# The last row of decays of blocks 0 to 3, stored and loaded back through GpSimd's DMA queue instead of SyncE's

## The chip, the cores and the metric

The kernel runs on one core of one Trainium2 chip. A core has TensorE (PE in the profile) for matrix products, VectorE (DVE), ScalarE (ACT), GpSimd (POOL) and SyncE (SP), which issues DMAs, and 16 DMA engines which move the data. Each engine works through its own instructions in program order and waits at semaphores for the others. Times are device microseconds of one execution; a kernel's time is the median of its runs.

## The reference

Gated linear attention, one step at a time, and then a feed-forward layer with a squared ReLU on its output:

```python
# q, k, v, alpha: (4, 8, 768, 48) float32, alpha in 0.8 to 1.0
for t in range(S):
    state = alpha[:, :, t, :, None] * state + einsum('bhd,bhe->bhde', k[:, :, t], v[:, :, t])
    y[:, :, t] = einsum('bhd,bhde->bhe', q[:, :, t], state)
x = y.transpose(0, 2, 1, 3).reshape(3072, 384)
h = maximum(x @ w_in, 0.0)        # w_in (384, 2048)
out = (h * h) @ w_out             # w_out (2048, 384)
```

The two weight matrices arrive as float64.

## The kernel before

**Blocks.** The sequence of 768 steps is cut into 6 chunks of 128, for 4 batch entries: 24 blocks, numbered n = 4c + b for chunk c of batch entry b. A block holds 128 steps by 8 heads by 48 channels. Its steps in the program have short names. `load` brings in alpha, q, k and v (line 109, 192 KB each). `ln` takes the logarithm of alpha on ACT (line 244); `cs` sums it along the chunk by a matmul with a triangle (line 265); `eb` and `ei` (lines 276 and 280, ACT) give b, the decay from the start of the chunk to each step, and its inverse; `mq` and `mk` multiply q by b and k by the inverse (line 284, DVE). `qT`, `kT` transpose on PE, `qc`, `kc` copy the results out of PSUM. `sc` makes the scores (line 372) and `kv` the sums of k and v (line 395) on PE; `am` masks the scores (line 380) and `us` adds the state (line 406) on DVE. `ya` and `yb` are the two halves of the output y of two blocks (line 352, PE); `ev` copies y into x (line 515, DVE and ACT in turn).

**The last row.** The next chunk's state is the sum so far times the last row of b, channel by channel. That row lies along one partition and is needed as columns, one channel per partition. So it goes through memory: `bl` (line 297) stores the row of 384 floats, 1.5 KB, into a small DRAM tile `row`; `br` (line 303) loads it back in two DMAs of 48 x 4 single floats each (0.8 KB) into the tile `last`, which has room for four blocks. `st` (lines 420 and 421, DVE) uses it: line 421 multiplies by `last`. All 20 blocks that have a successor do this, and all of these DMAs are issued by SP, among its loads. b has two buffers, so `eb` of block n waits until `bl` of block n-2 is done reading.

**Order.** The kernel is scheduled by hand. Blocks 0 to 3 (GB = 4) follow a list of step names (lines 851 to 860); each engine's program has them in the order of the list. The part with the first `bl` and `br`:

```python
ln0 cs0 ei0 mk0 warm0 eb0 bl0 mq0 kT0 load0v kc0 ln1 qT0 load2a load2k cs1
eb1 qc0 mq1 sc0 bl1 kv0 qT1 load1v ei1 mk1 load2q load3a kT1 ln2 qc1 load3k
cs2 br0 am0 kc1 eb2 sc1 weights0 br1 us0 kv1 zeros2 bl2 load2v am1 ei2 us1
load3q ya0 ln3 cs3 yb0 eb3 weights1 mk2 ei3 load3v mq2 qT2 st0 ev0 kT2
```

`zeros` are matmuls without use that fill PE's waits. `weights` loads an eighth of a weight matrix (line 126 or 130, 768 KB); `first`, `middle`, `second` convert it from float64 on DVE (lines 153, 157; 175, 179, 182) and ACT (lines 166, 169). `ha` and `hb` are the first feed-forward matmuls (line 805). The other blocks are woven into the feed-forward work by cost and due time; the feed-forward matmuls are at lines 622, 701 and 805.

**Queues.** SP's DMAs take eight semaphores in turn, so a DMA of SP is issued only when the one eight places before it has landed. GpSimd has memsets and masks at the start (to line 212, `last`) and then carries only a wait between `ya` and `yb` (line 456): it waits for the end of `ya`'s matmuls and then lets `yb` begin.

Of the kernel before, what the change touches and what calls it, by code (L numbers as in the profile page):

```python
# [17 lines left out]
GB = 4  # L18
# [7 lines left out]
def kernel(  # L26
# [12 lines left out]
    nc = tc.nc  # L39
    B, H, S, D = q.shape  # L40
    C = 128
# [171 lines left out]
    last_t = [last[:, i, :] for i in range(4)]  # L213
    dram = ctx.enter_context(tc.tile_pool(name="dram", bufs=1, space=bass.MemoryType.DRAM))
    rows_t = [dram.tile([1, H * D], FP32, name=f"row{n}") for n in range(NBLK)]
# [14 lines left out]
    blk = [{} for _ in range(NBLK)]  # L230
# [51 lines left out]
    def scaled(x, n, factor):  # L282
        t = tile_of(x, n)[:, :, 0:D]
        nc.vector.tensor_tensor(
            out=t, in0=t, in1=factor.rearrange("a (h d) -> a h d", h=H), op=ALU.mult
        )
# [4 lines left out]
    def mk(n):  # L291
        scaled("k", n, blk[n].pop("inv"))

    def bl(n):

        if n // B < NCH - 1:
            nc.sync.dma_start(out=rows_t[n], in_=blk[n]["b"][C - 1 : C, :])

    def br(n):
        if n // B < NCH - 1:  # L300
            row = rows_t[n].rearrange("a (p e d) -> (a d) e p", e=2, d=D)
            for e in range(2):
                nc.sync.dma_start(out=last_t[n % 4][64 * e : 64 * e + D, :], in_=row[:, e])  # L303

    def turned(x, n):
        rows = tile_of(x, n).rearrange("a h d -> a (h d)")
# [530 lines left out]


    steps = {f.__name__: f for f in (ln, sp, cs, eb, ei, mq, mk, bl, br, qT, qc, kT, kc, ev)}
    steps["sc"], steps["kv"], steps["am"] = scores, state_sums, masked  # L840
    steps["us"], steps["st"] = sums_copied, next_state
# [132 lines left out]
    for g in range(1, NG):  # L974
        events = []
        if g + 1 < NG:
            n = GB * (g + 1) + 2
# [4 lines left out]
        if g == 1:  # L982
# [5 lines left out]
            n = min(AT["k0"], AT["k1"])  # L988
# [41 lines left out]
```

## Time and profile before

| | us |
|---|---|
| median of 3 runs (522.41 to 522.86) | 522.62 |
| span of the profiled execution, first to last instruction | 520.6 |
| PE busy | 510.8 |
| DVE busy | 366.0 |
| ACT busy | 313.0 |
| POOL busy | 5.4 |

The profile is one execution. "Busy" is the sum of an engine's instructions; SPq and POOLq in the timelines are the queues of SP and POOL, in which the issue of a DMA or a wait is an instruction of its own. A timeline line gives the start, the length, the engine, the line of the kernel, the operation and what it writes and reads; in brackets is the engine's idle time just before it and what ended it. The chain of work goes back from the last instruction to whatever released each step. A matmul's end is modelled, not measured.

### The profile page before, as it was taken

How to read it: one execution, taken by the hardware profiler on the slowest of the kernel's cores; microseconds unless marked ns; L12 is line 12 of the kernel's file. 1: busy time of each engine (PE TensorE's matmuls, PEld its weight loads, DVE VectorE, ACT ScalarE, POOL GpSimd, SP SyncE). 2: the span in 40 equal slices, each digit the busy share in tenths (PEclk: the TensorE clock that was granted, in tenths of full speed). 3: DMA queues.
4: the chain of work that ended last, by engine and by line, in shares of the span. 5: the costliest groups of instructions: out<-in, count | busy, mean ns of one | idle time of the engine just before them, and what ended most of it. 6: DMA issues, size and time to landing. Idle time of an engine off the chain costs nothing.

```text
span 520.6 us, 12925 instructions
## 1 busy us (share of the span) xinstructions
PE 510.8 (98%) x5276; PEld 418.2 (80%) x5276; DVE 366.0 (70%) x631; ACT 313.0 (60%) x650; POOL 5.4 (1%) x29
## 2 busy tenths in 40 slices
PE   7989999999999999999999999999999999999997
PEld 4754455668887668988899988899988899988997
DVE  4798989979978787867597476587465476363861
ACT  4668785677888594575963275963275763164620
POOL 4000000000000000000000000000000000000000
PEclk9999999999999999999999999999999999999999
DMA  9999687244686787898884788964673534898201
GB/s 161 209 278 213 196 240 218 60 114 176 224 200 196 195 246 198 264 317 206 195 248 148 251 246 198 230 187 150 231 255 126 179 126 151 268 340 293 70 0 62
DMA packets 140995, 102.36 MB, mean 197 GB/s; under 512 B 111476, under 2 KB 114568, under 8 KB 140936
## 3 DMA queue, kind: packets, MB, share of 16 engines
q1 hardware_dynamic: 140936, 101.53, 68.3%
q8 instruction: 42, 0.69, 0.6%
q14 instruction: 17, 0.14, 0.1%
HBM read 84.18 MB, written 17.33 MB: 195 GB/s over the span
## 4 chain that ended last, share of the span: by engine, by line
PE 93%; DVE 2%; SPq 2%; DMA 1%; issue 1%; POOL 1%; ACT 0%; POOLq 0%; DVEq 0%
PE o L701 41%; PE h L622 32%; PE h L805 7%; PE y L352 4%; PE T L482 2%; PE sckv L372 2%; PE sckv L395 2%; PE cs L265 1%; DMA qk_lent<-in_q_dram 1%; SPq L303 1%; SPq L109 1%; PE cs L268 1%; PE cs L269 1%; DVE x L515 0%; DVE w_in L182 0%
## 5 line engine op out<-in xcount | busy, mean ns | idle before, releaser
L622 PE MATMUL h<-xa,wb 128*128 128x512 f32 x240 | 68.2, 392 | 0.0
L622 PE MATMUL h<-xl,wl 128*128 128x512 f32 x240 | 67.9, 391 | 0.0
L622 PE MATMUL h<-xd,wd 128*128 128x512 f32 x240 | 67.3, 396 | 0.0
L515 ACT COPY x<-y 32x256 f32<-32x256 f32 (+2 forms) x132 | 47.2, 366 | 25.4 <-PE y L352 20.1
L547 DVE TENSOR_TENSOR hid<-h,hid 128x512 f32<-128x512 f32 x40 | 27.6, 689 | 45.5 <-PE h L622 45.4
L701 PE MATMUL o<-wb,ha 128*128 128x384 f32 x160 | 54.6, 342 | 0.0
L701 PE MATMUL o<-w_out,hid 128*128 128x384 f32 x160 | 54.0, 491 | 0.0
L701 PE MATMUL o<-wd,hd 128*128 128x384 f32 x304 | 53.8, 334 | 0.0
L701 PE MATMUL o<-wl,hl 128*128 128x384 f32 x160 | 53.5, 335 | 0.0
L639 ACT ACTIVATE h<-h 128x512 f32<-128x512 f32 x40 | 23.3, 582 | 49.7 <-PE h L622 49.7
L622 PEld LDWEIGHTS h<-xl,wl 128*128 128x128 f32 x240 | 45.1, 188 | 10.0 <-DVE xl L547 0.4
L701 PEld LDWEIGHTS o<-wd,hd 128*128 128x128 f32 x304 | 52.7, 188 | 0.3 <-DVE osb L737 0.3
L622 PEld LDWEIGHTS h<-xa,wb 128*128 128x128 f32 x240 | 44.6, 188 | 9.3 <-ACT xa L596 0.2
L622 PEld LDWEIGHTS h<-xd,wd 128*128 128x128 f32 x240 | 44.2, 188 | 9.2
L701 PE MATMUL o<-wb,hx 128*128 128x384 f32 x144 | 48.7, 338 | 0.0
L701 PE MATMUL o<-wl,hx 128*128 128x384 f32 x144 | 48.1, 334 | 0.0
L701 PEld LDWEIGHTS o<-w_out,hid 128*128 128x128 f32 x160 | 29.8, 190 | 19.3
L637 ACT ACTIVATE hid<-h 128x512 f32<-128x512 f32 x40 | 24.0, 600 | 34.6 <-PE h L622 34.5
L805 PE MATMUL h<-x,w_in 128*128 128x512 f32 (+1 forms) x108 | 43.6, 552 | 1.2 <-ACT x L515 1.2
L596 ACT ACTIVATE ha<-hid 128x512 fp32r<-128x512 f32 x40 | 25.6, 639 | 25.5 <-DVE hx L547 16.1
L805 PEld LDWEIGHTS h<-x,w_in 128*128 128x128 f32 x108 | 19.9, 190 | 21.1 <-issue 17.2
L547 DVE TENSOR_TENSOR hl<-hid,ha 128x512 fp32r<-128x512 f32 x40 | 27.5, 688 | 10.1 <-ACT ha L596 10.1
(114 smaller groups left out, 879.7 us busy)
## 6 DMA issues: line engine op xcount, KB each, us to landing
wd<-do SPq DMA_DIRECT2D x36, 384.0 KB, 3.7
wl<-lo SPq DMA_DIRECT2D x34, 384.0 KB, 4.0
wl<-li SPq DMA_DIRECT2D x32, 384.0 KB, 3.5
wd<-di SPq DMA_DIRECT2D x32, 384.0 KB, 3.9
raw<-in_moe_w_in_dram SPq DMA_DIRECT2D x8, 768.0 KB, 5.6
raw<-in_moe_w_out_dram SPq DMA_DIRECT2D x8, 768.0 KB, 5.6
v_in<-in_v_dram SPq DMA_DIRECT2D x24, 192.0 KB, 4.7
out_dram<-osb SPq DMA_DIRECT2D x24, 192.0 KB, 1.9
```

Of the source, the lines that this page charges most:

```text
L352: ins = nc.tensor.matmul(out=ys[e][64 * half : 64 * half + D + G * e, m % 2, p // 2, t], lhsT=lhsT, rhs=rhs, start=(half, e) not in seen, ...
L372: nc.tensor.matmul(out=ps[e][HALF[h], 0, p, :], lhsT=ks[rows, p, HALF[h]], rhs=qs[rows, p, HALF[h]], start=True, stop=True, skip_group_che ...
L395: nc.tensor.matmul(out=ps[h][64 * e : 64 * (e + 1), 1, p, G:64], lhsT=tile_of("k", n)[HALF[h], 2 * p + e, :], rhs=tiles["v"][n % NV][HALF[ ...
L482: nc.tensor.transpose(out=ps[h][:, i, p, :], in_=rows[HALF[h], 128 * p : 128 * (p + 1)], identity=ident[HALF[h], HALF[h]],)
L515: copy(out=x[kk][to : to + m, t : t + 2], in_=blk[n]["y"][e][r : r + m, :, p // 2],)
L547: nc.vector.tensor_tensor(out=o, in0=x, in1=z, op=op)
L596: nc.scalar.activation(out=a, in_=x, func=AF.Copy, scale=NEAR)
L622: nc.tensor.matmul(out=acc["h", j], lhsT=here[w, "i", p][:, kk, jj * 128 : (jj + 1) * 128], rhs=x_parts[x][:, kk], start=start and kk == 0 ...
L637: nc.scalar.activation(out=hid[j], in_=x, func=AF.Copy, scale=E)
L639: nc.scalar.activation(out=x, in_=x, func=AF.Copy, scale=1.0 + E)
L701: nc.tensor.matmul(out=acc[t][:, 0:DM], lhsT=lhs[:, t * C : (t + 1) * C], rhs=rhs, start=start, stop=stop, skip_group_check=True,)
L805: nc.tensor.matmul(out=ps, lhsT=w[:, kk, c0 : c0 + 128], rhs=xT[g][kk][:, cols], start=(kk == 0), stop=(kk == KM - 1),)
```

## The change

`queue(n)` is GpSimd's queue for blocks 0 to 3 and SP's for the others; `bl` and `br` issue through it. Blocks 4 to 19 are as before, and so is the order of every other instruction on every engine.

```diff
+    def queue(n):
+        return nc.gpsimd if n < GB else nc.sync
+
     def bl(n):
 
         if n // B < NCH - 1:
-            nc.sync.dma_start(out=rows_t[n], in_=blk[n]["b"][C - 1 : C, :])
+            queue(n).dma_start(out=rows_t[n], in_=blk[n]["b"][C - 1 : C, :])
 
     def br(n):
         if n // B < NCH - 1:
             row = rows_t[n].rearrange("a (p e d) -> (a d) e p", e=2, d=D)
             for e in range(2):
-                nc.sync.dma_start(out=last_t[n % 4][64 * e : 64 * e + D, :], in_=row[:, e])
+                queue(n).dma_start(out=last_t[n % 4][64 * e : 64 * e + D, :], in_=row[:, e])
```

In GpSimd's program the order becomes: memset of `last`; bl0, bl1; br0 (two DMAs), br1 (two); bl2; the wait between ya0 and yb0; br2 (two); bl3; br3 (two); the wait between ya2 and yb2; then the other waits as before. Each `br` waits for its block's `bl` to land, each `bl` for ACT's `eb`. In the changed program bl is cut into 16 pieces of 24 floats, where SP's was one piece of 384.

## The prediction

> **What bounds the kernel now.** I read the page first, then the chain of work up to 90 us in order of time, then the timelines of DVE, SP and PE up to 40 us, then the DMA rates of those 40 us.
>
> The page:
>
> ```profile
> span 520.6 us, 12925 instructions
> PE 510.8 (98%) x5276; PEld 418.2 (80%) x5276; DVE 366.0 (70%) x631; ACT 313.0 (60%) x650; POOL 5.4 (1%) x29
> PE 93%; DVE 2%; SPq 2%; DMA 1%; issue 1%; POOL 1%; ACT 0%; POOLq 0%; DVEq 0%
> ```
>
> PE is busy for 510.8 of 520.6 us, so 9.8 us of idle PE are all that any reordering can win. The table by stretches puts 5.1 us of them before 35 us (PE 29.90 of 35.00); from 35.29 us on the chain is PE matmuls end to end, except one gap of 0.96 us at 203.09 us, called "issue". So the change can only win by bringing forward the moment at which PE starts its unbroken run, and everything moved lies before that moment. The chain there, in order of time (start, length, what):
>
> ```profile
> 9.45 0.25 SPq L297
> ...
> 13.12 2.31 SPq L303
> ...
> 18.25 5.06 DMA qk_lent<-in_q_dram
> 23.31 0.02 issue
> 23.33 0.10 DVE qk_lent L284
> ...
> 34.87 0.37 ACT x L515
> 35.25 0.04 issue
> 35.29 9.72 PE h L805 x26
> ```
>
> This looks as if the row transfers on SP (L297, L303) delay the load of block 3's q, and that load the whole start. DVE's timeline tells how much of it counts (start, length; idle before it and what ended it in brackets):
>
> ```profile
> 17.86 0.36 DVE L421 TENSOR_TENSOR s<-s,last 128x192 f32<-128x192 f32 x1 [1.41 <-DMA last<-row]
> 18.87 2.65 DVE L515 COPY x<-y 32x256 f32<-32x256 f32 x6 [0.65 <-PE y L352]
> ...
> 23.33 0.56 DVE L284 TENSOR_TENSOR qk_lent<-qk_lent,b 128x384 f32<-128x384 f32 x1 [0.28 <-DMA qk_lent<-in_q_dram]
> ```
>
> From 18.87 to 34.05 us DVE hardly stops. It waits 0.28 us for q3. **The bound of this stretch is DVE's run from 18.87 us**, so two things count: that 0.28 us, and what starts the run. The run starts after PE's y matmuls (18.12), which stand behind cs3 (PE 17.27, idle 0.47 before it, ended by ACT's logarithm of alpha of block 3), which waited for that load (ACT 16.70, idle 2.95, DMA).
>
> SP and the DMA rates (40 slices of 1 us):
>
> ```profile
> 4.43 1.15 SPq L109 DMA_DIRECT2D k_in<-in_k_dram  x1
> 6.89 0.31 SPq L297 DMA_DIRECT2D row<-b  x1
> 7.24 0.38 SPq L109 DMA_DIRECT2D v_in<-in_v_dram  x1
> ...
> 13.12 2.79 SPq L303 DMA_DIRECT2D last<-row  x2
> GB/s 0 13 218 206 191 192 187 157 132 223 204 182 193 187 185 92 15 143 356 331 233 122 122 324 377 221 214 244 376 288 196 351 346 238 101 142 358 393 360 364
> ```
>
> Loads run at about 190 GB/s, 1.0 us for each 192 KB. SP is stopped twice by the moved transfers. From 5.58 to 6.89 it waits for eb0; the load of v0 goes out only at 7.24, and the rate falls to 157 and 132 GB/s in the slices of 7 and 8 us. From 13.1 to 17.8 SP issues rows while the queue behind runs dry: 92 and 15 GB/s in the slices of 15 and 16 us.
>
> **The change part by part.** Twelve DMAs leave SP: 4 stores (L297, median 0.28 us of issue) and 8 loads (L303, median 0.44 us, together 5.6 us). POOL gets the same twelve behind its last memset, which ends at 6.21; after that POOL has no compute. No instruction of PE, DVE or ACT changes place.
>
> (1) v0 goes out at 5.6 instead of 7.24, so its data follow the sixth load without a gap. The gap is the shortfall of two slices: (190-157)/190 + (190-132)/190 = 0.48 us. The queue is full from there to 15 us, so v0, a2, k2, v1, q2, a3 and k3 all land some 0.5 us earlier. PE stood idle 0.45 us for v0 (10.31) and ACT 1.54 us for a2 (11.35). Link by link: kv0 9.8, qT1 10.4, kT1 10.9, cs2 11.4 (was 11.92), zeros 13.6, first half of y 15.1 to 16.3 (was 16.80), cs3 16.75 (was 17.27), second half 17.6, DVE's run 18.37. Gain 0.5 us. It can't be much more: mq1 and mk1 (9.46, 9.93) hang on eb1, which nothing moves. Bounds: 0.2 (half the gap is filled) and 0.55.
>
> (2) q3 lands earlier. The weights behind k3 start some 2 us sooner (no slices of 92 and 15 GB/s), so q3 lands near 20.5 instead of 23.31, when DVE is still in its copies. That takes 0.28 us off DVE. The rest of the chain's 5.06 us is worth nothing, because DVE was busy beside it. Next in line is L179, which needs ACT's L169 (ended 24.18, moves to 23.68): it would start at 23.9, so the 0.28 stays.
>
> (3) L421's wait for "last" (1.41 us) lay under the wait for PE's y and is worth nothing by itself.
>
> (4) On POOL I call T the mean time that one of these DMAs holds POOL. No row of this trace shows GpSimd issuing a DMA. The nearest is the same transfer on SP, 0.44 us; the ends are SP's shortest issue of it, 0.30, and its longest, 3.98 (that one waited). I take 0.44. The landing after the issue is taken as 2.0 us (row 3: issue ended 25.18, next L303 at 27.32; last of block 0: 15.91 to 17.86). Two deadlines: block 0's columns are there at 9.42+3T+2.0, needed at 18.0, so T may be 2.2. Block 3's end a chain of eleven DMAs after eb1 with two stores waited for: 9.42+11T+2x2.1+2.0 = 15.6+11T, needed by DVE's L421 at 36.87-0.78 = 36.1, so T may be 1.86. At 0.44 both are hidden, with nothing to pay. ACT's eb2 and eb3 now wait for POOL's stores, long landed by then (9 and 12 us against 12.9 and 17.7).
>
> The Trainium skill, DMA: Bandwidth & Descriptors, section "Latency and other measured facts", gives about 1 us to the first byte when GpSimd generates descriptors in software, against some 600 ns from SP; T of 1 would be an estimate by that page, and the sum stays the same by it. No run so far shows it.
>
> (5) The waits that GpSimd carries between the two halves of y (L456, 0.017 us each, the first at 16.9) now stand behind bl2 and br3 in POOL's program. The first of them releases PE's second half. If it waits for the seven DMAs before it, 9.42+6T must be below 16.4, so T may be 1.16; if it is done beside them, it costs nothing. At 0.44 neither costs.
>
> **Sum**: 0.5 + 0.28 = 0.78 us off the profiled 520.6, 519.8 us of span. The median of the runs shown is 522.62, 2.0 above the span; I carry the difference over: **521.8 us**. PE's clock row is 9 throughout, so clock plays no part.
>
> **Rivals.** *GpSimd's issue is slow (slower than before).* If T passes 1.86, each further 0.1 us of T brings block 3's columns 1.1 us late; DVE holds at L421 with the weight conversions behind it, which feed PE's L805. At T = 2.2 the columns land at 39.8, 3.7 us late, of which the waits of DVE on ACT at 42 to 52 us (0.53, 0.56, 1.20) give back some: about 523.5 to 525. At 2.5, 7 us late, up to 528. For it: these loads are 192 pieces of 4 bytes each, and nothing here shows how software handles them. Against it: it needs four times SP's time. With (5) in the strict form the loss starts at T of 1.16, and at T = 1.5 DVE's run starts 2.0 us later than forecast: 523.8.
> The Trainium skill, SBUF — State Buffer, section "SBUF: two separate sides", says that GpSimd cannot write descriptors while DVE runs an operation in a two-port mode; this would be part of this rival.
> Here L153 and L157 do 768 elements in 0.555 us where L284 takes 0.556 for 384; if such pairs (at 21.5 and 27.2) hold POOL, it is 2x1.1 us in all, and the limit for T falls from 1.86 to 1.66.
>
> *More is won.* The gap of 0.96 us at 203 us has no releaser; if it falls elsewhere and closes, 0.78+0.96 gives 520.9. It may also open elsewhere.
>
> *The transfers are hidden anyway.* If the lagging engine sets a3's landing, (1) wins nothing: the packet records show one 16 KB instruction packet of 1.46 us at 13.46, and a3's last part about 1.3 us behind the others. Then 0 to 0.28 is left: 522.3 to 522.6.
>
> **How the numbers follow.** 0.2% is 1.05 us, about what a measurement of this kernel can tell from no change. Forecast (0.3 to 1.05 us off, 521.6 to 522.3): 0.40. Hidden anyway: 0.13. More won, over 1.05 us: 0.25. Slow issue, slower by over 1.05 us: 0.22. So faster 0.25, same 0.53, slower 0.22. The range takes in the closed gap (520.9, rounded out to 520.8) and the slow issue up to T of some 2.3 (525.5); about 0.15 is left out, most of it above.
>
> **What would show it.** (1) right: no dip of the rate at 7 to 9 us, kv0 near 9.8, cs3 near 16.8, DVE's copies near 18.4. (2) right: no DMA wait ahead of DVE's L284 of q3, and L805's unbroken run near 34.5. (4) right: POOL's rows for the twelve DMAs below 1.8 us, block 0's columns landed before 17, L421 without a DMA wait near 36. Wrong: DVE idle at L421 for "last", or PE's second half of y waiting for POOL.

## The result and the profile after

The changed kernel takes **525.99 us** (five runs, 524.34 to 526.21) beside 522.62 us: a ratio of 1.0048, 95% interval 1.0036 to 1.0059. It is slower by 3.4 us, where 0.8 us less was forecast. Its profiled execution took 526.21 us with a span of 524.4 us, 3.8 us more than the span before. The lines of the code move: what was 297, 303, 352, 421, 456, 515 and 805 is now 300, 306, 355, 424, 459, 518 and 808.

The page of the changed kernel, the lines that were shown of before:

```profile
span 524.4 us, 12935 instructions
PE 512.2 (98%) x5276; PEld 420.3 (80%) x5276; DVE 365.7 (70%) x631; ACT 312.9 (60%) x650; POOL 12.2 (2%) x41
PE 93%; DVE 2%; SPq 2%; DMA 1%; issue 1%; ACT 0%; POOLq 0%; DVEq 0%
```

PE is idle for 12.2 us instead of 9.8, and busy for 1.4 us more with the same 5276 matmuls. So two things went wrong: PE stood still, and some of its work ran slower. Busy time that grows with no work added points at the clock.

The chain of waits of the changed kernel, in order of time (start, length, what):

```profile
11.03 5.90 DMA a_lent<-in_alpha_dram
16.93 0.02 issue
16.95 0.53 ACT a_lent L244
...
29.35 0.68 PE y L355 x28
30.03 1.65 issue
31.68 0.92 PE y L355 x16
...
33.83 14.04 PE h L808 x36
47.86 0.64 PE cs L265 x2
```

Before, the same cs stood at 45.01. The new thing is the 1.65 us in the middle of the y matmuls: "issue" says that PE waited for nothing that the profile shows. Here is PE's timeline at that place, first before and then after:

```profile
29.73 1.49 PE L352 MATMUL y<-am,v_in 64*48 64x64 f32 x64
```

```profile
29.61 0.42 PE L355 MATMUL y<-am,v_in 64*48 64x64 f32 x13
31.68 2.14 PE L355 MATMUL y<-am,v_in 64*48 64x64 f32 x51 [1.65 <-issue]
```

Up to the gap nothing is lost. DVE's timeline of the changed kernel:

```profile
17.27 0.36 DVE L424 TENSOR_TENSOR s<-s,last 128x192 f32<-128x192 f32 x1 [0.65 <-DMA last<-row]
19.12 2.65 DVE L518 COPY x<-y 32x256 f32<-32x256 f32 x6 [1.50 <-PE y L355]
...
23.22 0.55 DVE L284 TENSOR_TENSOR qk_lent<-qk_lent,b 128x384 f32<-128x384 f32 x1
...
33.88 2.67 DVE L518 COPY x<-y 32x256 f32<-32x256 f32 x6 [1.86 <-PE y L355]
```

Its first copies start 0.25 us later than before (18.87), the wait for q3 is gone, and its run reaches 32.03, some 0.1 us ahead of before. There it waits 1.86 us for the y that PE did not make: its second copies are 1.71 us late (33.88 against 32.17).

After that the same work takes longer. Here is PE's busy time in stretches of 3.413 us, laid along the steps in which this profile's clock changes (stretch; length, PE busy and its matmuls, granted clock, DMA share, GB/s):

```profile
24.65:28.06 3.41, 3.27 (x135) 1.00 0.71 186
28.06:31.48 3.42, 1.62 (x48) 1.00 1.13 304
31.48:34.89 3.41, 3.10 (x54) 0.50 1.03 195
34.89:38.30 3.41, 3.41 (x10) 0.50 0.88 290
38.30:41.72 3.42, 3.42 (x14) 1.00 0.99 262
```

The granted clock halves at 31.48, right after the stretch with the gap, and stays so for 6.83 us, two such stretches. In the profile of before it is 1.00 from 5.90 us to near the end. PE resumes at 31.68, so the y matmuls behind the gap ran at half clock too: 51 of them took 2.14 us, where the same 51 take 1.36 us at full clock (run 1 below). So of the 1.71 us some 0.93 belong to the gap and 0.78 to the clock, an estimate from these two rows. The count for the profiled execution: 0.93 us from the gap, 0.78 from the clock in y, 1.14 more until cs at 47.86 (2.85 in all; in runs 1, 2, 4, 5, 6 and 7, at full clock, cs shifts as DVE's second copies do, to 0.01 us, so this part is put down to the clock as well), 0.4 more at a second gap near 203 us (1.41 instead of 0.96; PE is 3.24 us late at its last matmul), and some 0.5 behind PE's last matmul: 3.8.

**Where the gap comes from.** The packets of the trace hold one kind that the prediction looked at only once: the instruction queue, 16 KB at a time, by which PE gets its program. The third of them ran from 26.47 to 27.72 us before, and from 28.97 to 29.98 after. PE stood still from 30.03, and started again 1.7 us behind the packet's end. What came ahead of the late packet is the third load of weights (`weights2`, 384 pieces of 2 KB): SP begins to issue it at 22.17 now and at 25.23 before (and is done at 25.07 and 25.77), because these row steps no longer stand in front of it on SP (before):

```profile
22.08 1.05 SPq L303 DMA_DIRECT2D last<-row  x2
23.23 0.39 SPq L109 DMA_DIRECT2D v_in<-in_v_dram  x1
23.67 1.51 SPq L297 DMA_DIRECT2D row<-b  x1
25.23 0.54 SPq L126 DMA_DIRECT2D raw<-in_moe_w_in_dram  x1
```

The experiments ask whether that is the cause, or GpSimd's transfers themselves are.

### The profile page after: what moved, and what is told of

Its sections match the earlier page's. It is cut to its first block, busy times and chain, and to the rows that moved or that the text cites. A ratio compares the mean times of both kernels' runs of the same rounds, so it can differ in the third digit from the quotient of the medians.

```text
span 524.4 us, 12935 instructions
## 1 busy us (share of the span) xinstructions
PE 512.2 (98%) x5276; PEld 420.3 (80%) x5276; DVE 365.7 (70%) x631; ACT 312.9 (60%) x650; POOL 12.2 (2%) x41
## 4 chain that ended last, share of the span: by engine, by line
PE 93%; DVE 2%; SPq 2%; DMA 1%; issue 1%; ACT 0%; POOLq 0%; DVEq 0%
PE o L704 41%; PE h L625 32%; PE h L808 8%; PE y L355 5%; PE T L485 2%; PE sckv L375 2%; SPq L109 2%; PE sckv L398 2%; DMA a_lent<-in_alpha_dram 1%; PE cs L265 1%; PE cs L269 1%; PE cs L268 1%; DVE x L518 0%; DVE power L153 0%; DVE am L383 0%
## 5 line engine op out<-in xcount | busy, mean ns | idle before, releaser
L808 PE MATMUL h<-x,w_in 128*128 128x512 f32 (+1 forms) x108 | 45.0, 573 | 0.0
L808 PEld LDWEIGHTS h<-x,w_in 128*128 128x128 f32 x108 | 21.8, 205 | 19.5 <-issue 17.2
```

The lines of the kernel that those rows point to most:

```text
L808: nc.tensor.matmul(out=ps, lhsT=w[:, kk, c0 : c0 + 128], rhs=xT[g][kk][:, cols], start=(kk == 0), stop=(kk == KM - 1),)
```

## The experiments

Each run stands beside runs of the kernel before on the same chip: 522.66 us in the first group, 522.84 in the second, 522.75 in the third. In some of the records on these runs, theory F or W is the instruction fetch, and P or G says that GpSimd's transfers do the harm.

**1. No rows at all.** The kernel before, without the stores and loads of the rows of blocks 0 to 3:

```diff
-        if n // B < NCH - 1:
+        if GB <= n and n // B < NCH - 1:
```

(in `bl` and in `br`.)

> The kernel before with no row transfers at all for blocks 0 to 3 (line 421 then multiplies by the zeros that last was set to, so the output of the later chunks lacks the carried state). SP is freed as in the change, and GpSimd issues nothing. Theory F (SP, freed, keeps the DMA engines so full that PE's third 16 KB instruction fetch comes late, PE runs dry in the middle of y, and the clock is halved for some 7 us after it): a gap of 1 us or more with no releaser inside y near 30 us, a mean granted clock of 0.990 to 0.998, 524 to 526.3 us, as after the change. Rival P (the transfers issued by GpSimd, or their queue, are what costs): no gap, clock 1.000, at or a little below the kernel before, 521.8 to 522.7 us.

Measured: 523.36 us (522.47 to 525.33), ratio 1.0015 [1.0003, 1.0027], between the two ranges expected: both theories missed the time. With less work it is not faster. PE's timeline:

```profile
29.23 0.42 PE L352 MATMUL y<-am,v_in 64*48 64x64 f32 x13
31.04 1.36 PE L352 MATMUL y<-am,v_in 64*48 64x64 f32 x51 [1.39 <-issue]
```

The same gap at the same place with no transfer of GpSimd in the program; the fetch ran from 28.43 to 29.66. So GpSimd is not needed for it. In the profiled run the clock stayed at 1.00, and PE's cs was 0.29 us later than before, where these y matmuls began 0.5 us sooner (29.23 against 29.73): at full clock the gap costs some 0.8 us, an estimate from these two differences. Of its ten runs, six had a mean clock of 1.000 and took 522.47 to 523.55 us (mean 522.9); four had 0.993 to 0.997 and took 523.71 to 525.33 (mean 524.3).

**2. The rows on both queues.** SP's rows stay, and GpSimd does the same twelve DMAs again into memory that nothing reads:

```diff
+        if n < GB:
+            nc.gpsimd.dma_start(out=spare_t[n], in_=blk[n]["b"][C - 1 : C, :])
...
+                nc.gpsimd.dma_start(out=spare[64 * e : 64 * e + D, n, :], in_=row[:, e])
```

> The kernel before, with SP's row transfers as they are, and the same twelve transfers issued by GpSimd once more, into memory that nothing reads. Theory F: SP is held back as before, so no gap inside y near 30 us, clock 1.000, 522.3 to 523.0 us, as before. Rival P: the gap and the lower clock of the change, 524 to 526 us.

Measured: 523.71 us (523.06 to 525.15), ratio 1.0020 [1.0010, 1.0031]. The fetch is on time (26.74) and there is no gap. But the loads are late: cs3 at 17.68 instead of 17.27, DVE's first copies at 19.27 instead of 18.87. DVE's second copies are 0.46 us late (32.63). So GpSimd's twelve transfers, beside SP's own, cost about 1 us, half of it by late loads and none by the fetch; where the other half goes was not followed. Both theories missed this.

**3. Only blocks 0 and 1 on GpSimd.**

```diff
+    def queue(n):
+        return nc.gpsimd if n < 2 else nc.sync
```

> The change for blocks 0 and 1 alone; blocks 2 and 3 stay on SP, where the store of block 3 and its load wait again for ACT and for the store's landing. Theory F: SP is ahead until some 22 us and held back at the rows of blocks 2 and 3, so the third fetch is on time or nearly; gap under 0.7 us, 522.0 to 523.5 us. Rival P: eight of the twelve transfers' cost is left (six DMAs), about half of the loss, 524 to 525 us.

Measured: 524.91 us (524.11 to 526.0), ratio 1.0042 [1.0026, 1.0057]. The fetch theory had expected a packet nearly on time; it came at 29.01, PE's gap was 1.39 us, and the clock was halved for one stretch of 3.41 us. Its time was missed because I had taken the rows of blocks 2 and 3 to hold `weights2` back by themselves. The packets say no: the load's first piece moved at 25.63. This run let the other theory stand.

**4. v0's load ahead of block 0's store.** The kernel before with one entry of the list moved:

```diff
-        ln0 cs0 ei0 mk0 warm0 eb0 bl0 mq0 kT0 load0v kc0 ln1 qT0 load2a load2k cs1
+        ln0 cs0 ei0 mk0 warm0 load0v eb0 bl0 mq0 kT0 kc0 ln1 qT0 load2a load2k cs1
```

> The kernel before with the load of v0 issued ahead of the store of row 0, so at 5.6 instead of 7.24 us; nothing else moves. This is step (1) of the prediction alone. By the prediction: kv0 at 9.8, DVE's copies of y at 18.4, 522.1 us (0.5 us less). By what the trace after shows (v0 issued at 5.66, and PE still waits for it until 10.45): the loads run at the DMA engines' rate anyway, kv0 at 10.2 to 10.5, copies at 18.7 to 19.1, 522.4 to 522.9 us.

Measured: 522.59 us (522.28 to 522.97), ratio 0.9998 [0.9989, 1.0008]. kv0 10.33 (10.31 before), cs3 17.25 (17.27), DVE's copies 18.85 (18.87). It takes the stop at 5.6 us out, and with it nothing is gained. This is the prediction's step (1) by itself.

**5. The change, with the weights held back.** All rows of blocks 0 to 3 stay on GpSimd; SP issues `weights2` and `weights3` later in the list, and `load4a` sooner:

```diff
-        weights2 qT3 sc2 load4q qc3 kv2 second0 am2 br3 first1 sc3 weights3 us2
-        load4a kv3 am3 us3 load4k middle1 ha1 second1 ya2 yb2 ev2 weights4 first2
+        qT3 sc2 load4q load4a qc3 kv2 second0 am2 br3 first1 sc3 weights2 us2
+        kv3 am3 us3 load4k weights3 middle1 ha1 second1 ya2 yb2 ev2 weights4 first2
```

> The change (rows of blocks 0 to 3 on GpSimd's queue), with the issues of weights2 and weights3 moved further back in the list of early work, so that SyncE issues weights2 after sc3, at about the time at which it did in the kernel before. Theory W: the late instruction fetch of PE (28.97 to 29.98 us, where it was 26.47 to 27.72) comes from the weights load that the change sends 3 us sooner. It expects the fetch at 26 to 27 us, no gap of over 0.5 us in the y matmuls near 31 us, a granted clock of 1.0 from 4 to 125 us in the profile, and 522.3 to 523.3 us: what is left over the kernel before is what GpSimd's transfers cost the loads. Rival G: the transfers of GpSimd's queue delay the fetch and the work whatever the weights do. It expects the gap and the lower clock as in the change, 524 to 526 us.

Measured: 523.29 us (522.98 to 523.41), ratio 1.0007 [0.9998, 1.0016]. The fetch is at 26.76. PE's timeline at the place of the gap:

```profile
29.72 1.49 PE L355 MATMUL y<-am,v_in 64*48 64x64 f32 x64
31.14 1.56 PE L808 MATMUL h<-x,w_in 128*128 128x256 f32 x6
```

All 64 matmuls in one piece, as before (29.73). The clock stays at 1.00 to near the end; DVE's second copies start at 32.16 (32.17 before) and PE's chain at 35.28 (35.29). An edit that touches no row and no transfer of GpSimd leaves 0.45 of the 3.4 us.

**6. The kernel before, with the weights sent early.** The opposite: all rows on SP, and only `weights2` put ahead of br2:

```diff
-        zeros2 zeros2 zeros2 kc2 first0 mk3 middle0 kT3 mq3 br2 load4v qc2 kc3 bl3
-        weights2 qT3 sc2 load4q qc3 kv2 second0 am2 br3 first1 sc3 weights3 us2
+        zeros2 zeros2 zeros2 kc2 first0 mk3 middle0 kT3 mq3 weights2 br2 load4v qc2 kc3 bl3
+        qT3 sc2 load4q qc3 kv2 second0 am2 br3 first1 sc3 weights3 us2
```

> The kernel before, all rows on SyncE's queue, with only the issue of weights2 moved some six entries forward in the list of early work. No transfer of GpSimd is in it. Theory W (the weights load, where it flows when PE's third instruction fetch is wanted, holds the fetch up): fetch at 27.6 to 29 us instead of 26.47, a gap of 1 us or more in the y matmuls near 30 us, a clock below 0.999 in some runs, 523 to 525 us. Rival G (GpSimd's transfers are the cause): fetch at 26 to 27 us, no gap, 522.4 to 522.9 us.

Measured: 523.30 us (522.95 to 524.79), ratio 1.0009 [0.9999, 1.0018]; four of ten runs at a mean clock of 0.995 to 0.997. The fetch moved to 28.29, and PE's timeline has the gap:

```profile
29.75 0.42 PE L352 MATMUL y<-am,v_in 64*48 64x64 f32 x13
31.01 1.36 PE L352 MATMUL y<-am,v_in 64*48 64x64 f32 x51 [0.84 <-issue]
```

The mechanism is there, with a gap a little shorter than the 1 us expected, and the time lies in the expected range at its low end; the ratio alone would not tell it from no change.

**7. No rows, with the weights held back.** The edits of 1 and 5 together.

> The kernel without the stores and loads of the last rows of blocks 0 to 3 on any queue (line 421 multiplies by zeros instead, so the state carried into blocks 1 to 3 and 1 of the computation is left out), and with weights2 and weights3 held back as in the run with the change. Beside the run without rows and without the hold (523.36 us, gap of 1.39 us, fetch at 28.43) it is the limit of what could be won by taking the rows off SyncE. Theory W: fetch at 26 to 27 us, no gap, clock 1.0, 521.7 to 522.5 us. Rival: the freed slots of SyncE bring another transfer into the fetch's way or the gap at 203 us takes the gain back: 522.6 to 523.4 us.

Measured: 522.25 us (521.97 to 522.70), ratio 0.9986 [0.9977, 0.9996], where run 1 has 1.0015. The fetch moved only part of the way, to 27.68, and a gap of 0.54 us is left, which was not expected. With no rows to move at all, and that gap left, 0.6 us are won: there was little to win here.

**The fetch in all runs.** From the packet records: the third 16 KB instruction packet, the third load of weights, and how many of its 384 pieces had started before that packet. (PE's gap is that in the y matmuls near 30 us.)

| run | third load, first to last piece | pieces ahead of the fetch | fetch starts | gap |
|---|---|---|---|---|
| before | 26.62 to 29.97 | 0 | 26.47 | none |
| 4, v0 first | 26.37 to 29.90 | 2 | 26.43 | none |
| 2, both queues | 26.89 to 30.43 | 0 | 26.74 | none |
| 9, short stall (below) | 26.63 to 29.94 | 0 | 26.39 | none of "issue" |
| 8, long stall (below) | 27.02 to 30.46 | 0 | 26.94 | none of "issue" |
| 5, change, weights held | 28.38 to 31.15 | 0 | 26.76 | none |
| 7, no rows, weights held | 26.80 to 30.61 | 24 | 27.68 | 0.54 |
| 6, weights early | 25.43 to 27.86 | 384 | 28.29 | 0.84 |
| 1, no rows | 25.14 to 28.10 | 385 (one of the next) | 28.43 | 1.39 |
| 3, blocks 0 and 1 | 25.63 to 28.60 | 384 | 29.01 | 1.39 |
| 10, change again | 26.22 to 29.19 | 364 | 28.97 | 1.10 |
| after | 25.72 to 28.77 | 384 | 28.97 | 1.65 |

Either the fetch starts about when the load's first pieces do (0.9 us behind the first of them in run 7), or it stands behind the whole load or nearly all of it. Where it starts at 28.3 us or later, PE stands still for 0.84 to 1.65 us; how long also depends on when PE gets there (30.03 in the changed kernel, 30.35 in run 10, with the fetch at 28.97 in both). The Trainium skill, DMA: Bandwidth & Descriptors, section "Queues, rings and completion order", says that a DMA engine takes turns between the queues that have work for it, and changes only at the end of a packet, typically of some 9 to 17 descriptors and at most 64. 384 pieces spread evenly over 16 engines would be 24 each; by that page this is an estimate of less than the largest packet, so that a whole load ahead of the fetch could fit it, but of more than a typical one. The records here do not name the engine of a piece, so why the fetch waits is not shown.

**8 and 9. A stall without the fetch.** The kernel before, every transfer in its place, with GpSimd copying block 3's masked scores onto themselves (five times in run 8, three in run 9), so that PE's y matmuls wait:

```diff
+        for _ in range(5 if n == 3 else 0):
+            nc.gpsimd.tensor_copy(out=am_h(n)[:, :, 1], in_=am_h(n)[:, :, 1])
```

> The kernel before, every transfer where it was, with five copies by GpSimd of the masked scores of block 3 onto themselves after DVE wrote them (29.2 us): the last y matmuls of the first pair of blocks in the second step wait for them, so that PE stands still near 30 us for some 1.5 us or more (how long one copy takes is not known from these traces). Theory C (PE's standing still here is what halves the granted clock afterwards, for a whole number of windows of 3.41 us): clock 0.991 to 0.997 in part of the runs, and these are 1.4 to 3.4 us above the runs with clock 1.000, beside what the stall itself costs. Rival N (the fall of the clock belongs to the transfers or the late fetch, not to the idle time): clock at 0.999 to 1.000 in all runs, and the time above the kernel before by the stall alone, at most its length.

> As the run with five copies, with three. Theory C: a stall of about three fifths of the other's, a lower clock in fewer runs or none. Rival N: clock at 0.999 to 1.000, time above the kernel before by at most the stall.

Measured: 526.88 us (526.64 to 528.01), ratio 1.0084 [1.0069, 1.0099], and 525.33 us (524.71 to 526.51), ratio 1.0058 [1.0041, 1.0075]. One copy takes 1.03 to 1.06 us, so the stalls were longer than meant: 4.26 and 2.31 us. The fetch is on time in both (26.94, 26.39). The clock fell in every run (0.992 or 0.993 in run 8, 0.993 to 0.997 in run 9). Here are the stretches of run 9, and then those of run 8:

```profile
29.56:32.97 3.41, 1.10 (x48) 1.00 1.13 295
32.97:36.38 3.41, 3.28 (x40) 0.50 0.90 189
36.38:39.80 3.42, 3.42 (x16) 1.00 1.04 369
```

```profile
30.73:34.14 3.41, 0.00 (x0) 1.00 1.12 294
34.14:37.56 3.42, 2.47 (x50) 0.50 0.83 208
37.56:40.97 3.41, 3.41 (x10) 0.50 1.07 355
```

So the clock halves after idle PE with neither the late fetch nor a moved transfer. GpSimd's copies, which run in the meantime, are in none of the change and runs 3 and 10; idle PE is what they all have in common. What is not shown is the price: no run of 8 or 9 kept its clock, and both times (4.1 and 2.6 us above before) would be about what the stall alone could cost. For run 9 the expectation of fewer runs with a lower clock was wrong, since the stall was longer than planned.

Here are all profiles up to some 43 us, taken in stretches of 3.413 us in step with the clock's changes and leaving out the first ones up to 8 us. Where PE is busy for 0.00, 1.10, 1.62, 1.65 or 1.84 us of a stretch at full clock (runs 8, 9, after, 3, and 10 below), the next one runs at half clock; with 2.02 us (run 1) or more, none does. Behind a stretch at half clock came a second one where PE was busy for 2.47 or 3.10 us of the first (run 8, after), and none where it was busy for 3.28 us or more. One of the stretches left out does not fit: in run 5, from 4.20 to 7.61 us, PE is busy for 1.73 us and the clock stays at 1.00. So busy time alone is not shown to be the rule. Where the stretches begin differs from run to run (4.17 us after the span's start in one, 6.84 in another). A gap of the same 1.39 us lay in one stretch with PE's shorter waits before it in run 3 (1.65 us busy), and without most of them in run 1 (2.02).

**10. The change again.**

> The change as it is, again, beside the same runs of the kernel before. Theory W with C: the instruction fetch again at 28.5 to 29.5 us, a gap of 1.3 to 1.7 us in the y matmuls in each profile; the time follows the mean clock of the run, about 526 us at 0.992, 524.5 us at 0.995 to 0.997, and 523 to 523.5 us where a run should keep 1.000. Rival G: the time does not follow the clock.

Measured: 525.20 us (524.57 to 526.18, four runs), ratio 1.0049 [1.0034, 1.0064]. Fetch at 28.97, a gap of 1.10 us (shorter than expected), half clock for one stretch. Over the nine runs of this kernel in both groups, a mean clock of 0.992 goes with 525.81 to 526.21 us, and 0.995 to 0.997 with 524.34 to 524.65. The one run at 1.000 took 524.57, though, 1.1 us more than expected of it: about 1.8 us of the loss are there without the clock, by this one run. That is near the count above without its two clock terms: 0.93 + 0.4 + 0.5 us. Gap and clock both cost. Where the clock's stretches begin seems to set how much (runs 1 and 3); no run varies that by itself.

No version of these beats both kernels. The best that computes everything is the kernel before, or run 4, which is the same within 0.1%.

## Why the prediction was wrong

**What failed** is the Sum, at three places: step (1), its main term of 0.5 us, which is worth nothing; the weights that step (2) sends sooner, which it counts at no cost, and which held up PE's instruction fetch (some 0.93 us); and the sentence that PE's clock row is 9 throughout, "so clock plays no part" (some 1.92 us). The moment that the prediction wants to bring forward, the start of PE's unbroken run, did come sooner (33.83 against 35.29), but with 36 matmuls left up to cs instead of 26, because PE had stood still before, and at half clock at first.

**Step (1), 0.5 us from v0's earlier issue: wrong, −0.25 us.** v0 went out at 5.66, as predicted. kv0 stood at 10.45 (predicted 9.8, before 10.31), cs3 at 17.53 (16.75; 17.27), DVE's copies at 19.12 (18.4; 18.87). The rate rows show why. Here are the 40 slices of 1 us of the changed kernel:

```profile
GB/s 0 15 203 199 195 192 196 163 173 207 184 165 210 168 162 132 106 318 380 278 192 254 342 288 211 58 143 373 346 241 315 312 266 156 89 303 369 221 338 335
```

The dip at 7 to 9 us is smaller, as predicted (163 and 173 instead of 157 and 132). But the load queue had been catching up: the count of 192-byte pieces landed is ahead of before by some 210 at 9 us and 120 at 10, and some 65 behind by 12. Before, the slices behind the dip ran at 223 and 204 GB/s; I took 190 as a ceiling. The dip, followed by a faster stretch, cost nothing downstream, and run 4 measures that: cs3 is 0.02 us earlier, and the time is the same. The 0.25 us lost instead come with GpSimd's transfers: run 2, which adds them and moves nothing, shows 0.4, and run 1, which frees SP without them, has cs3 at 17.15, 0.1 us ahead.

**Step (2), 0.28 us at q3: right.** No wait ahead of DVE's row at 23.22; DVE was some 0.1 us ahead at 32.03 in spite of its late start. The sentence in it that was read as a gain only, "The weights behind k3 start some 2 us sooner", is where the loss came in. The third load's pieces started 0.9 us sooner, in front of the fetch instead of just behind it.

**Step (3), the wait for "last" is worth nothing: right.** It went from 1.41 to 0.65 us (17.27) and nothing hung on it.

**Step (4): T near enough to the 0.44 us taken, the landings far off.** GpSimd's timeline in the changed kernel:

```profile
6.34 0.63 POOL L300 DMA_DIRECT2D row<-b  x1
9.47 0.50 POOL L300 DMA_DIRECT2D row<-b  x1 [2.49 <-ACT b L276]
11.34 1.20 POOL L306 DMA_DIRECT2D last<-row  x2 [1.36 <-DMA row<-b]
...
25.70 1.17 POOL L306 DMA_DIRECT2D last<-row  x2 [5.53 <-DMA row<-b]
```

0.52 us per store and 0.59 per load (medians), far from the 1.86 at which it was to decide. So the rival of the slow issue is out; that the time lies in the range that it gave is chance, since the cause is another. The landing is slower than the 2.0 us I took: GpSimd's stores land 3.5 to 5.8 us after their issue, its loads 1.9 to 6.9. From its issue to the first piece moved there are 1.4 (second store) to 3.9 us (last load). The page DMA: Bandwidth & Descriptors of the Trainium skill, in "Latency and other measured facts", gives about 1 us to the first byte; every one of these is above it. Columns of block 0 landed at about 17.2, not "before 17", still in time. Block 3's landed at 32.9, where 15.6 + 11T with T = 0.44 gives 20.4: also in time, for DVE's L424 at 38.58, but by much less than reckoned. None of GpSimd's issues ran beside L153 or L157 (21.81, 27.09), so nothing here shows whether these would hold it up.

**Step (5), the wait between the halves of y: right.** POOL's wait is 0.03 us in the chain (32.62).

**The rivals.** "More is won" said of the gap at 203 us that it "may also open elsewhere", and gave that no price. That is what happened, with a wait of the same kind: an "issue" gap in y matmuls, near an instruction packet. At 203 us, in the kernel before, PE resumed at 204.05 behind a packet that ended at 202.65; that gap had a cause that could have been read, and it would have pointed at the fetch at 26.47, whose pieces of weights began at 26.62.

**What stays open.** Run 5 is 0.45 us above the kernel before (interval −0.1 to +0.8), of which its profile shows 0.4 in the gap at 203 us (1.36). Why that gap is anything from 0.77 to 1.50 us in different profiles was not tried. Why the fetch waits for nearly the whole load is not shown. How the loss splits between gap and clock is an estimate from one profile, and from the spread among runs of one program.

## What to carry to other kernels

A transfer taken off a queue lets everything behind it on that queue go sooner, and that can be worse: ask of each transfer that is brought forward what it will run into, and put PE's instruction packets on that list. An "issue" gap in a run of small matmuls is a reason to look up the instruction queue's packets, and a load can be held back by moving its place in the order by hand. Before a gap in transfers is counted as a gain, see whether the rate behind it is higher than the average: then it was being made up already.

## What the runs showed of the hardware

- PE comes back 1.4 to 1.7 us after its instruction packet has landed (29.98 to 31.68, 205.91 to 207.33 after; 202.65 to 204.05 before). Small matmuls such as those of y pass fast: 64 of them take 1.49 us.
- The clock halved for whole stretches of 3.41 us after a stretch in which PE was idle for about half or more (busy for 1.84 us or less); the one early stretch of run 5 is an exception. The Trainium skill, TensorE: Matmul & The Clock Gate, Part 1, gives the length of the window as 3413 ns and says that its phase is free, and the traces agree (segments of 3.41 and 6.83 us). Its section "HAM oscillation — how this bites in real kernels" gives the rule of no idle gaps over some 3.4 us; here gaps of 1.1 to 1.65 us were enough (runs 3, 10 and after).
- The Trainium skill, Runtime: NRT & Kernel Launch, section "Instruction fetch mechanics", says that crossing a block of 16 KB is mostly hidden. Here PE had at most two waits of this kind in a profile: one with the late fetch near 30 us, of 0.54 to 1.65 us, and one near 203 us, of 0.77 to 1.50 us in the different profiles.
- GpSimd's copies slow DVE down while they run. In run 8, beside them:

```profile
29.87 1.33 DVE L175 SCALAR_TENSOR_TENSOR power<-raw,power 128x768 uint32<-128x768 uint32 x1
31.12 1.36 DVE L179 SCALAR_TENSOR_TENSOR w_in<-upper,w_in 128x768 f32<-128x768 uint32 x1
32.51 1.25 DVE L182 TENSOR_TENSOR w_in<-w_in,power 128x768 f32<-128x768 f32 x1
```

These take 0.95, 0.95 and 0.96 us in the profiles of before and of the changed kernel. GpSimd's DMA issues did not: in the changed kernel L182 took 0.96 us beside the last of them (25.70).
